# Loads of u and v in runs of 1024 B instead of 2048 B, and the turn of u in two transfers

## The chip, the cores and the metric

The kernel runs on one core of one Trainium2 chip. A core has TensorE (PE, matrix products into PSUM), VectorE (DVE), ScalarE (ACT), GpSimd (POOL) and SyncE (SP), and sixteen DMA engines that move data between the chip's memory (DRAM here) and SBUF. SP, ACT and POOL issue transfers, each into a queue of its own; the profile calls SP's queue q1, ACT's q10 and POOL's q0. The metric is the device time of one execution in microseconds (us), the median of several runs. A profile shows one such execution.

## The reference

The inputs are u and v (8 x 3136 x 256), z (8 x 3136 x 64), three projections of 256 columns in one matrix, a filter (3136 x 256) and an output matrix. All are float32. For each of the 8 batches:

```
scores = z @ z.T / 3136
x      = u * (relu(scores)**2 @ v)
x1, x2, x3 = x @ w_proj            # 256 columns each
x2c    = irfft(rfft(x2) * rfft(filter))   # along the 3136 rows
out    = (x1 * x2c * x3) @ w_out
```

The 3136 x 3136 weights of each batch are by far the largest product.

## The kernel before

The 3136 rows of a batch are taken as 64 x 49, so that the Fourier transform falls into two stages. They are held as 25 row blocks of 128 rows (the last of 64), two of the 49 columns to a block. The output rows of a batch are worked on in seven chunks of 512, 512, 512, 512, 512, 256 and 320 columns (4, 4, 4, 4, 4, 2 and 3 row blocks); 8 batches make 56 chunks.

For each chunk TensorE makes scores of pairs of row blocks against the chunk into PSUM (from zT_t), ACT or DVE applies relu (into R_t) and the square (into A_t), and TensorE weighs v with A_t. The sums go to PSUM, where DVE multiplies them with u, turned, into xT_t (L1975). Scores are symmetric: a block of weights that a later chunk needs is not made again but turned. SP issues a transposing transfer (DMA_TRANSPOSE) from A_t to M_t, M2e_t or M2o_t (L1848), and a later chunk weighs with those. An A_t is free when its turn and its products are done.

From xT_t come the three projections. The middle one goes through the Fourier stages by way of DRAM: SP stores s_t and gs_t to the spectrum buffers and loads them again (spec_in_t, conv_in_t). At the end of a batch the gates, the convolution and the output matrix give ost_t, which SP stores to out_dram.

The loads: u, v and z come from DRAM as float32 and are cast to bfloat16 by the transfer itself. Only POOL issues such loads. A load fills 64 of the 128 partitions, one for each of 64 row groups, with up to four row blocks side by side. `load_rows` (L644) does it for v, into a tile v_t that holds the 25 blocks of one batch, 256 columns each; `v_at` (L641) is the column of a block, with 16 unused columns between chunks. `cast_u` (L627) does it for u, one chunk at a time, into un_t, with `cast_rows` (L618). Each chunk has two loads of u, one for each half of the partitions, and two pieces of v of the next batch. Each of them follows a small copy on POOL into `tick`, which waits for a given piece of work, so that loads are spread over time. u is loaded two chunks ahead.

The turn of u: SP issues one transposing transfer per chunk from un_t to uT_t (`load_uT`, L1561, issued at L1565), which DVE reads at the end of the chunk. uT_t and un_t have two buffers each, M_t one, M2e_t and M2o_t one each, A_t eight.

The order of the work comes from a planner that runs when the program is built. It takes costs and due times for each task; the order of TensorE's work and the choice between ACT and DVE are written out in two strings. [...]

Of the kernel before, what the change touches and what calls it, by code (L numbers as in the profile page):

```python
# [11 lines left out]
P = 128  # L12
F32 = mybir.dt.float32
BF16 = mybir.dt.bfloat16
# [4 lines left out]
N1 = 64  # L19
# [367 lines left out]
def kernel(  # L387
# [10 lines left out]
    nc = tc.nc  # L398

    B, S, D = u.shape  # L400
# [3 lines left out]
    NT = (N2 + 1) // 2  # L404
    NC = len(CHUNKS)
    C0 = [sum(CHUNKS[:i]) for i in range(NC)]
    QUART = S // 4
    T0 = [x // P for x in C0] + [NT]
    tiles = [list(range(T0[c], T0[c + 1])) for c in range(NC)]
    home = {t: c for c in range(NC) for t in tiles[c]}  # L410
    VW = NT * D + 16 * (NC - 1)
    inv_s2 = 1.0 / float(S) ** 2
    h_scale = 2.0 / float(S)

# [23 lines left out]
    PS = bass.MemoryType.PSUM  # L438
    zT_p = Pool("zT", 2, [P, NT * P], BF16)
    uT_p = Pool("uT", 2, [P, 4, 2, P], BF16)  # L440
    un_p = Pool("un", 2, [P, 4, D], BF16)
    zn_p = Pool("zn", 1, [P, 8, dqk], BF16)
    zd_p = Pool("zd", 1, [P, 8, 2, dqk], BF16)
    v_p = Pool("v16", 2, [P, VW], BF16)
    R_p = Pool("R", 3, [P, 2, 512], F32)
# [130 lines left out]
    def on(engine, emit, cost, deps=(), takes=(), **kw):  # L576
        return job(None, lambda e: emit(), {engine: cost}, deps, takes, **kw)
# [18 lines left out]
    def rows_n1(x):  # L596
        return x.rearrange("(n1 n2) d -> n1 n2 d", n2=N2)

    def runs(lo, hi):
        got = []  # L600
        for c in range(NC):
            a, b = max(lo, T0[c]), min(hi, T0[c + 1])
            if a < b:
                got.append((0, a, b, NT - T0[c + 1] + a - T0[c]))
        if lo < min(hi, NT - 1):
            got.append((1, lo, min(hi, NT - 1), NT + lo))
        return got
# [10 lines left out]
    def cast_rows(t, src, t0, t1, twice=False, js=(0, 1)):  # L618
        x = rows_n1(src)
        if twice and t1 == NT:  # L620
            nc.gpsimd.dma_start(out=t[N1:P, t1 - 1 - t0, :], in_=x[:, END_N2, :])
        for j, lo, hi, n2 in runs(t0, t1):
            if j not in js:
                continue
            nc.gpsimd.dma_start(out=t[ds(j * N1, N1), lo - t0 : hi - t0, :], in_=x[:, n2 : n2 + hi - lo, :])  # L625

    def cast_u(b, c, js=(0, 1)):  # L627
        if 0 in js:
            u_nat[b, c] = un_p.tile()
        t = u_nat[b, c]  # L630
        if c == NC - 1 and 0 in js:
            nc.gpsimd.memset(t[N1:P, T0[c + 1] - 1 - T0[c], :], 0.0)
        cast_rows(t, u[b], T0[c], T0[c + 1], js=js)

    def await_x(xt):
        nc.gpsimd.tensor_copy(tick[:], xt["t"][0:1, 1, 0:1])
# [2 lines left out]
        nc.gpsimd.tensor_copy(tick[:], live[un][0:1, 0:1])  # L639

    def v_at(t):  # L641
        return t * D + 16 * home[t]

    def load_rows(t, src, t0, t1, js=(0, 1)):  # L644
        r = rows_n1(src)
        for j, lo, hi, n2 in runs(t0, t1):
            if j not in js:
                continue
            for c in range(home[lo], home[hi - 1] + 1):
                a, b = max(lo, T0[c]), min(hi, T0[c + 1])  # L650
                nc.gpsimd.dma_start(  # L651
                    out=t[ds(j * N1, N1), ds(v_at(a), (b - a) * D)],
                    in_=r[:, n2 + a - lo : n2 + b - lo, :].rearrange("p t d -> p (t d)"),
                )
        if t1 == NT and 1 in js:
            nc.gpsimd.dma_start(out=t[N1:P, ds(v_at(NT - 1), D)], in_=r[:, END_N2, :])

    def row(t, i):
        return t[:, ds(v_at(i), D)]
# [6 lines left out]
    for t0, t1 in zip(z_cuts, z_cuts[1:]):  # L666
        for j, lo, hi, n2 in runs(t0, t1):
            (nc.scalar if j else nc.sync).dma_start(
                out=zf[lo // ZF][ds(j * N1, N1), lo % ZF : lo % ZF + hi - lo, :], in_=zr[:, n2 : n2 + hi - lo, :]
# [28 lines left out]
    nc.gpsimd.iota(k0v[:, 0:25], pattern=[[N1, 25]], base=0, channel_multiplier=0)  # L698
    nc.gpsimd.iota(k0v[:, 25:50], pattern=[[-N1, 25]], base=S // 2, channel_multiplier=0)
    load_rows(v16[0], v[0], 0, 8)  # L700
    u_nat = {}
    load_rows(v16[0], v[0], 8, 16)
    cast_u(0, 0)
    load_rows(v16[0], v[0], 16, NT)
    wp16 = const.tile([P, 2, 3 * D], BF16, name="wp16")
    nc.gpsimd.dma_start(out=wp16[:], in_=moe_w_proj.rearrange("(t p) n -> p t n", p=P))
    cast_u(0, 1)
    wo16 = const.tile([P, 2, D], BF16, name="wo16")
    S2_AT = 30.0
# [40 lines left out]
    def after(task, at):  # L750
        task.ready = max(task.ready, at)
        return task
# [12 lines left out]
    for i, (t0, t1) in enumerate(zip(z_cuts, z_cuts[1:])):  # L765
        step_ = -(-(t1 - t0) // -(-(t1 - t0) // 8))
        for g0 in range(t0, t1, step_):
# [15 lines left out]
            n = nt * dqk  # L783
# [6 lines left out]
            w = min(nt * P, S - g0 * P)  # L790
# [367 lines left out]
    def c_quads(i, n=1):  # L1158
        return n * (1 if i else 2) * c_pe(2 * D) + 0.01
# [4 lines left out]
    def add_quads(mm, ev, cost, deps, takes, wide=True):  # L1164
        box = {}

        def go():
            box["p"] = take_pair()
            mm(box["p"])

        a = pe("Q", go, cost, deps, [pair_slots, *takes])
        evs = []
        for h in ((0, 1),) if wide else (0, 1):
            x = slice(0, 2) if wide else slice(h, h + 1)
            e_ = job(None, lambda e, x=x: ev(e, x, box["p"][:, x, :]), both(2 * D * (1 + wide)), [a])
            e_.frees.append((a, 0))
            evs.append(e_)
        a.holders = len(evs)
        return a, evs
# [18 lines left out]
    for j0 in range(0, NJ, 4):  # L1198
        ld, ibox = load_spec(DF, j0, 4, puts, LATE_F)
        for i in range(2):  # L1200
# [7 lines left out]
            a, evs = add_quads(mm, ev, c_quads(j0 // 2 + i), [*s2_done, ld], [])  # L1208
# [340 lines left out]
    uT = {}  # L1549
# [8 lines left out]
    def u_tiles(c):  # L1558
        return -(-CHUNKS[c] // P)

    def load_uT(b, c, deps):  # L1561
        def go():
            uT[b, c] = uT_p.tile()
            n = -(-CHUNKS[c] // P)
            nc.sync.dma_start_transpose(  # L1565
                out=uT[b, c][:, 0:n].rearrange("p t h j -> p (t h) j"),
                in_=u_nat[b, c][:, 0:n].rearrange("p t d -> p (t d)"),
            )

        made = cu[b, c]  # L1570
        if not isinstance(made[0], Task):
            t = after(on("SP", go, 1.3, deps, [uT_p.slots], moves=0.2 * u_tiles(c), late=LATE_U), made[1])
            t.frees.append((Held(un_p.slots, made[0]), 0))
        else:
            t = on("SP", go, 1.3, [*deps, *made], [uT_p.slots], moves=0.2 * u_tiles(c), late=LATE_U)
            t.frees.append((made[0], 0))
        t.clogs = True
        u_tasks[b, c] = t
# [17 lines left out]
    def casts_at(b, c):  # L1596
# [60 lines left out]
        if x < len(slots):  # L1657
            box = []

            def go_u(tick_, js):  # L1660
                a = on(
                    "POOL", lambda: cast_u(*slots[x], js), 0.55 * len(js), [tick_, *box], [] if box else [un_p.slots],
                    moves=0.264 * len(js) * u_tiles(slots[x][1]), late=LATE_CAST,
                )
                box.append(a)
                if 1 in js:
                    cu[slots[x]] = box[0], a
                    load_uT(*slots[x], [])

            got += [lambda t_, j=j: go_u(t_, (j,)) for j in range(2)]  # L1670
# [48 lines left out]
    def parts(un):  # L1719
        b, c, k = un  # L1720
        pair = plans[b, c][k][1]
        return [(t, c) for t in pair] + ([(NT - 1, SHARE[c])] if c in SHARE and pair == (NT - 1,) else [])
# [157 lines left out]
    for gi, g in enumerate(groups):  # L1880
        deps = []
        for un in g:
            b, c, k = un
            if b == 0:
                hi = max((plans[b, c][k][1][-1] + 1) * P, C0[c] + CHUNKS[c])
# [19 lines left out]
        for i, un in enumerate(g):  # L1905
            b, c, k = un
            cw = CHUNKS[c]
            pair = plans[b, c][k][1]
            rows, n = P, len(parts(un))
# [54 lines left out]
            if last:  # L1964
# [48 lines left out]
                if calls or b == 0 and c < 3:  # L2013
# [8 lines left out]
                    for i, call in enumerate(calls):  # L2022
                        k = (i * (len(mine) + 1)) // len(calls) if mine else 0
# [6 lines left out]
    for gi, got in ends_at.items():  # L2030
        for b, c in got:
            q_, un, _ = short[b, c]
# [37 lines left out]
```

## Time and profile before

| | |
|---|---|
| time, median of 3 runs | 951.24 us (949.6 to 953.36) |
| the profiled execution, its own time | 946.01 us |
| its span, first to last instruction | 944.1 us |
| mean granted TensorE clock | 0.997 |
| TensorE, DVE, ACT, POOL busy | 97%, 89%, 87%, 26% of the span |
| packets in flight, q1 and q0 | 70.1% and 26.4% of sixteen DMA engines' time |
| moved by DMA | 170.70 MB, mean 181 GB/s |

Lines of the profile name the kernel's line, the engine, what is written and read, the count, the busy time and mean length, and the idle time of the engine just ahead with what ended it. "SPq" is an issue of a transfer by SP: the time for which SP was taken up, not the transfer's own. "The chain" follows the work that ended last back to the start. In the lines on transfers "KB" is one transfer's size in SBUF, and the last number the median time from issue to landing. Shares of the DMA queues add up the times of all packets; packets overlap on an engine, so they can exceed 100%.

### The profile page before, as it was taken

How to read it: one execution, taken by the hardware profiler on the slowest of the kernel's cores; microseconds unless marked ns; L12 is line 12 of the kernel's file. 1: busy time of each engine (PE TensorE's matmuls, PEld its weight loads, DVE VectorE, ACT ScalarE, POOL GpSimd, SP SyncE). 2: the span in 40 equal slices, each digit the busy share in tenths (PEclk: the TensorE clock that was granted, in tenths of full speed). 3: DMA queues.
4: the chain of work that ended last, by engine and by line, in shares of the span. 5: the costliest groups of instructions: out<-in, count | busy, mean ns of one | idle time of the engine just before them, and what ended most of it. 6: DMA issues, size and time to landing. Idle time of an engine off the chain costs nothing.

```text
span 944.1 us, 30298 instructions
## 1 busy us (share of the span) xinstructions
PE 914.1 (97%) x12423; PEld 557.1 (59%) x12423; DVE 838.5 (89%) x1116; ACT 819.7 (87%) x953; POOL 248.8 (26%) x585
## 2 busy tenths in 40 slices
PE   8999999999999999999999999999999999999986
PEld 3446565566555666556665665666665666666654
DVE  8987899998888998999888988989988999899785
ACT  7968988999889988888989998889988999899573
POOL 5244223231322322223121321333123140101030
PEclk9999999999999999999999999999999999999999
DMA  9999799978999889998899989999889989897867
GB/s 155 162 181 181 117 179 184 181 150 182 170 217 201 146 181 192 209 156 159 190 183 215 176 155 200 173 184 174 183 172 207 221 138 196 193 216 132 193 189 241
DMA packets 331643, 170.70 MB, mean 181 GB/s; under 512 B 242886, under 2 KB 307142, under 8 KB 331504
## 3 DMA queue, kind: packets, MB, share of 16 engines
q1 hardware_dynamic: 301624, 131.98, 70.1%
q0 software_dynamic: 29168, 35.13, 26.4%
q8 instruction: 97, 1.59, 0.7%
q10 hardware_dynamic: 712, 1.66, 0.6%
q14 instruction: 42, 0.34, 0.1%
HBM read 90.26 MB, written 53.05 MB: 152 GB/s over the span
## 4 chain that ended last, share of the span: by engine, by line
PE 77%; DMA 10%; DVE 6%; ACT 3%; issue 2%; SPq 1%; POOL 0%; ACTq 0%; DVEq 0%; POOLq 0%
PE ps_s L516 77%; DMA M_t<-A_t 4%; DMA out_dram<-ost_t 1%; ACT R_t L1919 1%; DMA M_t<-spec_in_t 1%; DVE xh L1357 1%; ACT A_t L1928 1%; DVE yT_t L1462 1%; DVE A_t L1930 1%; DMA v_t<-spec 1%; DMA spec<-gs_t 1%; DMA M2e_t<-A_t 1%; ACT gs_t L582 1%; DVE R_t L1357 1%; DMA spec_in_t<-spec 0%
## 5 line engine op out<-in xcount | busy, mean ns | idle before, releaser
L516 PE MATMUL ps_s<-A_t,v_t 64*128 64x512 bf16 (+5 forms) x4766 | 516.1, 352 | 0.9 <-DVE A_t L1930 0.7
L516 PEld LDWEIGHTS <-v_t 64*128 64x128 bf16 (+1 forms) x6528 | 306.4, 98 | 187.7 <-PE ps_s L516 19.3
L1919 ACT ACTIVATE R_t<-ps_s 128x1024 f32<-128x1024 f32 (+3 forms) x359 | 336.9, 962 | 47.4 <-PE ps_s L516 43.8
L1928 ACT ACTIVATE A_t<-R_t 128x1024 bf16<-128x1024 f32 (+2 forms) x281 | 271.8, 993 | 15.3 <-DMA M_t<-A_t 6.3
L1930 DVE SCALAR_TENSOR_TENSOR A_t<-R_t 128x1024 bf16<-128x1024 f32 (+3 forms) x211 | 233.6, 1123 | 21.6 <-ACT R_t L1919 12.1
L516 PE MATMUL ps_s<-zT_t 64*128 64x512 bf16 (+5 forms) x1186 | 192.2, 351 | 3.6 <-DVE gate_t L1256 2.1
L1921 DVE TENSOR_SCALAR R_t<-ps_s 128x1024 f32<-128x1024 f32 (+4 forms) x153 | 170.2, 1123 | 20.9 <-PE ps_s L516 10.4
L639 POOL COPY tick<-A_t 1x1 bf16<-1x1 bf16 x159 | 56.2, 354 | 428.0 <-ACT A_t L1928 264.2
L516 PE MATMUL ps_s<-xT_t,wp 64*128 64x512 bf16 (+3 forms) x976 | 124.7, 352 | 0.1
L516 PE MATMUL ps_s<-M_t,v_t 64*128 64x512 bf16 (+4 forms) x860 | 97.2, 353 | 3.2 <-DMA M_t<-A_t 2.4
L516 PEld LDWEIGHTS <-zT_t 64*128 64x128 bf16 (+1 forms) x1219 | 69.1, 97 | 51.7 <-issue 8.2
L582 ACT ACTIVATE x_t<-ps_s 128x1024 bf16<-128x1024 f32 (+3 forms) x75 | 69.5, 928 | 22.8 <-PE ps_s L516 22.5
L1357 DVE TENSOR_TENSOR xh<-xh,H 128x1024 bf16<-128x1024 bf16 x120 | 81.7, 685 | 2.3 <-ACT xh L582 1.4
L1256 DVE TENSOR_TENSOR gate_t<-ps_s,x_t 128x512 bf16<-128x512 f32 (+2 forms) x112 | 64.4, 617 | 12.4 <-PE ps_s L516 9.0
L1462 DVE TENSOR_TENSOR yT_t<-ps_s,gate_t 128x1024 bf16<-128x1024 f32 (+2 forms) x53 | 56.9, 1078 | 14.3 <-PE ps_s L516 14.1
L1975 DVE TENSOR_TENSOR xT_t<-ps_s,uT_t 128x512 bf16<-128x512 f32 (+2 forms) x112 | 64.0, 613 | 6.3 <-PE ps_s L516 5.8
L516 PEld LDWEIGHTS <-wp 64*128 64x128 bf16 (+1 forms) x976 | 48.0, 96 | 29.7 <-PE ps_s L516 2.0
L516 PE MATMUL ps_s<-wp,xT_t 64*128 64x256 bf16 (+2 forms) x944 | 64.2, 266 | 0.8 <-ACT R_t L1919 0.7
L516 PE MATMUL ps_s<-wo,yT_t 64*128 64x256 bf16 (+2 forms) x904 | 62.1, 266 | 2.2 <-DVE yT_t L1462 1.0
L625 POOL DMA_DIRECT2D un_t<-in_u_dram x112 | 57.9, 518 | 17.4 <-issue 15.6
L651 POOL DMA_DIRECT2D v_t<-in_v_dram x112 | 58.2, 524 | 14.1 <-issue 10.4
L516 PEld LDWEIGHTS <-xT_t 64*128 64x128 bf16 (+1 forms) x944 | 44.1, 97 | 19.3 <-issue 1.5
(156 smaller groups left out, 905.7 us busy)
## 6 DMA issues: line engine op xcount, KB each, us to landing
out_dram<-ost_t SPq DMA_DIRECT2D x60, 256.0 KB
spec_in_t<-spec SPq DMA_DIRECT2D x56, 192.0 KB
spec<-gs_t SPq DMA_DIRECT2D x56, 192.0 KB
v_t<-in_v_dram POOLq DMA_DIRECT2D x80, 128.0 KB, 4.8
un_t<-in_u_dram POOLq DMA_DIRECT2D x80, 128.0 KB, 4.4
spec<-s_t SPq DMA_DIRECT2D x40, 256.0 KB
conv_in_t<-spec SPq DMA_DIRECT2D x34, 256.0 KB
out_dram<-ost_t SPq DMA_DIRECT2D x18, 128.0 KB
```

The costliest lines, as they stand in the source:

```text
L516: got = nc.tensor.matmul(o, *args, **kw)
L582: got = nc.scalar.activation(out_, in_, AF.Copy)
L625: nc.gpsimd.dma_start(out=t[ds(j * N1, N1), lo - t0 : hi - t0, :], in_=x[:, n2 : n2 + hi - lo, :])
L651: nc.gpsimd.dma_start(out=t[ds(j * N1, N1), ds(v_at(a), (b - a) * D)], in_=r[:, n2 + a - lo : n2 + b - lo, :].rearrange("p t d -> p (t d)"),)
L1256: has_read(nc.vector.tensor_tensor(o[:, :, ::-1] if h == 0 else o, p, x, ALU.mult), p)
L1357: nc.vector.tensor_tensor(x[:, 1 - i], x[:, 0], h, ALU.mult)
L1462: has_read(nc.vector.tensor_tensor(yb["y"][:, :, 0:w], p, gates[b, c][:, :, 0:w], ALU.mult), p)
L1919: has_read(nc.scalar.activation(r, p, AF.Relu), p)
L1921: has_read(nc.vector.tensor_single_scalar(r, p, 0.0, ALU.max), p)
L1928: nc.scalar.activation(a, r, AF.Square, scale=1.0 / float(S))
L1930: nc.vector.scalar_tensor_tensor(a, r, inv_s2, r, ALU.mult, ALU.mult)
L1975: has_read(nc.vector.tensor_tensor(x[:, :, ::-1] if h == 0 else x, f, ut, ALU.mult), f)
```

## The change

The tile of a chunk of u, un_t, is now two groups of two row blocks with 16 unused columns after each group. The tile of v gets 16 unused columns after every second row block of a chunk. A load of four row blocks is still one transfer, but its run in SBUF is broken after two blocks: two runs of 512 bfloat16 elements, 1024 B, in each partition. The memory side is cut in the same way. Three row blocks now take two transfers, one of two blocks and one of one block. The turn of u works on one group at a time: two transfers for chunks of four or three row blocks, one for the chunk of two. The strings and the planner's costs are the same; so is the order of the instructions on TensorE, ACT and DVE.

```diff
-    VW = NT * D + 16 * (NC - 1)
+    starts = sorted(t for c in range(NC) for t in tiles[c][::2])
+    pads = {t: sum(x <= t for x in starts) - 1 for t in range(NT)}
+    VW = NT * D + 16 * len(starts)
...
-    un_p = Pool("un", 2, [P, 4, D], BF16)
+    un_p = Pool("un", 2, [P, 2, 2 * D + 16], BF16)
...
+    def u_part(t, lo, n):
+        return t[:, lo // 2, ds(lo % 2 * D, n * D)]
+
     def cast_u(b, c, js=(0, 1)):
...
-        cast_rows(t, u[b], T0[c], T0[c + 1], js=js)
+        x = rows_n1(u[b])
+        for j, lo, hi, n2 in runs(t0, T0[c + 1]):
+            if j not in js:
+                continue
+            k = (hi - lo) // 2
+            if k:
+                nc.gpsimd.dma_start(
+                    out=t[ds(j * N1, N1), 0:k, 0 : 2 * D],
+                    in_=x[:, n2 : n2 + 2 * k, :].rearrange("p (k t) d -> p k (t d)", k=k),
+                )
+            if (hi - lo) % 2:
+                nc.gpsimd.dma_start(out=u_part(t, hi - 1 - t0, 1)[ds(j * N1, N1)], in_=x[:, n2 + hi - lo - 1, :])
...
     def v_at(t):
-        return t * D + 16 * home[t]
+        return t * D + 16 * pads[t]
...
-                nc.gpsimd.dma_start(
-                    out=t[ds(j * N1, N1), ds(v_at(a), (b - a) * D)],
-                    in_=r[:, n2 + a - lo : n2 + b - lo, :].rearrange("p t d -> p (t d)"),
-                )
+                while a < b:
+                    m = 1 if (a - T0[c]) % 2 else min(2, b - a)
+                    k = max(1, (b - a) // 2) if m == 2 else 1
+                    out = t[ds(j * N1, N1), ds(v_at(a), k * (2 * D + 16))] if k > 1 else t[ds(j * N1, N1), ds(v_at(a), m * D)].unsqueeze(1)
+                    if k > 1:
+                        out = out.rearrange("p (k w) -> p k w", k=k)[:, :, 0 : 2 * D]
+                    nc.gpsimd.dma_start(
+                        out=out,
+                        in_=r[:, n2 + a - lo : n2 + a - lo + k * m, :].rearrange("p (k t) d -> p k (t d)", k=k),
+                    )
+                    a += k * m
...
-            nc.sync.dma_start_transpose(
-                out=uT[b, c][:, 0:n].rearrange("p t h j -> p (t h) j"),
-                in_=u_nat[b, c][:, 0:n].rearrange("p t d -> p (t d)"),
-            )
+            for k in range(0, n, 2):
+                m = min(2, n - k)
+                nc.sync.dma_start_transpose(
+                    out=uT[b, c][:, k : k + m].rearrange("p t h j -> p (t h) j"), in_=u_part(u_nat[b, c], k, m)
+                )
```

POOL at the start of the program, where v and u of the first batch are loaded ahead of the projections' matrix (wp), before and then now. A form like 64x1024 is partitions by elements; 64x2x512 is two runs of 512 elements in each partition. Counts at the end of a row are repeats.

```order
L651 DMA v_t<-in_v_dram 64x1024 x8
L625 DMA un_t<-in_u_dram 64x1024 x2
L651 DMA v_t<-in_v_dram 64x1024
L651 DMA v_t<-in_v_dram 64x512
L651 DMA v_t<-in_v_dram 64x768
L651 DMA v_t<-in_v_dram 64x1024
```

```order
L674 DMA v_t<-in_v_dram 64x2x512 x8
L645 DMA un_t<-in_u_dram 64x2x512 x2
L674 DMA v_t<-in_v_dram 64x2x512
L674 DMA v_t<-in_v_dram 64x512 x2
L674 DMA v_t<-in_v_dram 64x256
L674 DMA v_t<-in_v_dram 64x2x512
```

The order is the same; the load of 768 elements is now one of 512 and one of 256.

SP in the sixth batch, where a turn of u stands ahead of a store of s_t, two stores of the output and two turns of weights into M_t, before and then now. For a DMA_TRANSPOSE 128x8x128 is eight squares of 128 x 128, that is four row blocks of 256 columns.

```order
L1620 DMA_TRANSPOSE zT_t<-zd_t 128x8x128
L1565 DMA_TRANSPOSE uT_t<-un_t 128x8x128
L1028 DMA spec_1_60<-s_t 128x4x256
L1511 DMA out_dram<-ost_t 64x1024 x2
L1848 DMA_TRANSPOSE M_t<-A_t 128x8x128 x2
```

```order
L1645 DMA_TRANSPOSE zT_t<-zd_t 128x8x128
L1591 DMA_TRANSPOSE uT_t<-un_t 128x4x128 x2
L1052 DMA spec_1_60<-s_t 128x4x256
L1535 DMA out_dram<-ost_t 64x1024 x2
L1873 DMA_TRANSPOSE M_t<-A_t 128x8x128 x2
```

Nothing has changed its place; one more transfer stands ahead of the rest.

SP at the last turn of u, that of the last chunk, with the stores of the last spectrum but one ahead and the loads of the next one behind, before and then now.

```order
L1406 DMA spec_0_61<-gs_t 48x2048 x2
L1406 DMA spec_0_61<-gs_t 2x2048
L1565 DMA_TRANSPOSE uT_t<-un_t 128x6x128
L1077 DMA spec_in_t<-spec_1_60 40x2048 x4
L1091 DMA conv_in_t<-spec_0_61 128x4x256 x2
```

```order
L1430 DMA spec_0_61<-gs_t 48x2048 x2
L1430 DMA spec_0_61<-gs_t 2x2048
L1591 DMA_TRANSPOSE uT_t<-un_t 128x4x128
L1591 DMA_TRANSPOSE uT_t<-un_t 128x2x128
L1101 DMA spec_in_t<-spec_1_60 40x2048 x4
L1115 DMA conv_in_t<-spec_0_61 128x4x256 x2
```

The turn of three row blocks has become one of two blocks and one of one block, at the same place.

More of the change, by code (lines that the diff above doesn't have):

```diff
@@ L630, in cast_u @@
         t = u_nat[b, c]
+        t0 = T0[c]
         if c == NC - 1 and 0 in js:
-            nc.gpsimd.memset(t[N1:P, T0[c + 1] - 1 - T0[c], :], 0.0)
-        cast_rows(t, u[b], T0[c], T0[c + 1], js=js)
+            nc.gpsimd.memset(u_part(t, T0[c + 1] - 1 - t0, 1)[N1:P], 0.0)
+        x = rows_n1(u[b])
[10 more added lines that the diff above has]
+                nc.gpsimd.dma_start(out=u_part(t, hi - 1 - t0, 1)[ds(j * N1, N1)], in_=x[:, n2 + hi - lo - 1, :])
     def await_x(xt):
```

## The prediction

> **What bounds the kernel now.** I read the page first: busy shares, the two DMA queues, and the shares of the chain of waits.
>
> ```profile
> span 944.1 us, 30298 instructions
> PE 914.1 (97%) x12423; PEld 557.1 (59%) x12423; DVE 838.5 (89%) x1116; ACT 819.7 (87%) x953; POOL 248.8 (26%) x585
> ...
> q1 hardware_dynamic: 301624, 131.98, 70.1%
> q0 software_dynamic: 29168, 35.13, 26.4%
> ...
> PE 77%; DMA 10%; DVE 6%; ACT 3%; issue 2%; SPq 1%; POOL 0%; ACTq 0%; DVEq 0%; POOLq 0%
> PE ps_s L516 77%; DMA M_t<-A_t 4%; DMA out_dram<-ost_t 1%; ACT R_t L1919 1%; DMA M_t<-spec_in_t 1%; DVE xh L1357 1%; ACT A_t L1928 1%; DVE yT_t L1462 1%; DVE A_t L1930 1%; DMA v_t<-spec 1%; DMA spec<-gs_t 1%; DMA M2e_t<-A_t 1%; ACT gs_t L582 1%; DVE R_t L1357 1%; DMA spec_in_t<-spec 0%
> ```
>
> TensorE bounds it: 914.1 of 944.1 us busy, so all of its idle time together is 30.0 us. A change of loads can win at most part of that, and can lose more. Second comes the DMA: 26.4% and 70.1% of sixteen engines' time are packets in flight, and 10% of the chain, 94 us, are transfers. The casting loads are the smaller queue, q0, which GpSimd issues; the turns, the spectrum and the output go through q1, nearly all issued by SP.
>
> Then the chain in order of time (start, length, what), for the places where a transfer ends last.
>
> ```profile
> 17.57 10.96 DMA M_t<-spec_in_t
> ...
> 279.66 5.55 DMA out_dram<-ost_t
> ...
> 377.49 7.05 DMA M_t<-A_t
> ...
> 393.83 5.95 DMA out_dram<-ost_t
> 399.80 7.75 DMA M_t<-A_t
> ...
> 619.18 8.86 DMA M_t<-A_t
> ...
> 638.34 5.61 DMA spec<-gs_t
> ...
> 880.09 1.33 SPq L1565
> ...
> 884.00 4.56 DMA spec_in_t<-spec
> ```
>
> None of them is a load of u or v. They are what SP issues: turns of weights (M_t), spectra and outputs. So the loads matter through what they do to SP's transfers, and the turn of u (L1565) matters as something that stands in SP's queue ahead of these. In the row at 880.09 it is on the chain itself.
>
> **The change part by part.** It edits three things: the runs of the loads, their number on POOL, and the number of turns on SP.
>
> (1) Shorter runs. How the loads are issued (count, KB each, median us to landing), and what one stretch with long runs and one with shorter runs moved (q0: packets, MB, share of the sixteen engines; the first row is for 11 to 13 us, the second for 13 to 16 us, where q0 is nearly alone):
>
> ```profile
> v_t<-in_v_dram POOLq DMA_DIRECT2D x80, 128.0 KB, 4.8
> un_t<-in_u_dram POOLq DMA_DIRECT2D x80, 128.0 KB, 4.4
> v_t<-in_v_dram POOLq DMA_DIRECT2D x8, 96.0 KB, 4.2
> un_t<-in_u_dram POOLq DMA_DIRECT2D x8, 96.0 KB, 3.8
> ```
>
> ```profile
> q0 software_dynamic: 241, 0.40, 107.0%
> ```
>
> ```profile
> q0 software_dynamic: 517, 0.53, 105.7%
> ```
>
> Each 128 KB load fills 64 partitions with a run of 2048 B; now it is two of 1024 B. Each 96 KB load becomes 1024 and 512 B. That adds 160 x 64 + 16 x 64 = 11,264 runs. The price of one more run, from the two stretches: 1.070 x 16 x 2 us / 241 = 142 ns a packet at 0.40 MB / 241 = 1.66 KB, and 1.057 x 16 x 3 us / 517 = 98 ns at 1.03 KB. The line through both is 70 ns per KB and 26 ns per packet. By it the change adds 11,264 x 26 ns / 16 = 18.3 us of all sixteen engines, 1.9% of the span. From below the price is nothing, if time goes by bytes alone.
>
> [...]
>
> Where this lies on the path: mostly nowhere, since loads land 4 to 5 us after issue and are asked for two chunks ahead, and a chunk is 944.1 / 56 = 16.9 us. Without that cover the 18.3 us would count whole. There are two exceptions. At the start ten such loads of v, four of u and one of 96 KB are issued ahead of 17.57, where the chain waits 10.96 us for a turn: 15 x 64 x 26 ns / 16 = 1.6 us at most, 0 at least. I take **1.0**, nearer the measured line. And the chain's 94 us of transfers, slowed by 1.9% at most, lose 0 to 1.8; I take **0.5**, since most of them are issued while few loads are in flight.
>
> (2) Sixteen more loads on POOL (each 96 KB one is split in two). They take 16 x 0.518 us by the first row below, 8.3 us. POOL is busy 26%, so I count nothing; without that idle time it would be the 8.3.
>
> ```profile
> L625 POOL DMA_DIRECT2D un_t<-in_u_dram x112 | 57.9, 518 | 17.4 <-issue 15.6 <-DVE xT_t L1975 0.7 <-DVE xh L1362 0.3
> ...
> L1975 DVE TENSOR_TENSOR xT_t<-ps_s,uT_t 128x512 bf16<-128x512 f32 (+2 forms) x112 | 64.0, 613 | 6.3 <-PE ps_s L516 5.8
> ```
>
> The second row is the only reader of uT_t: of its 6.3 us of waiting 5.8 are for TensorE, none is put down to a turn. So a turn of u that ends later costs its reader nothing.
>
> (3) The turn of u is two transfers in 48 of 56 cases (all chunks but the one of 256 columns). SP issues in order. What a short turn costs it: the turn at 865.28 is that of the chunk of 256 columns, as large as the first half of the new ones.
>
> ```profile
> 865.28 1.20 SPq L1565 DMA_TRANSPOSE uT_t<-un_t  x1
> ...
> 881.53 2.80 SPq L1077 DMA_DIRECT2D spec_in_t<-spec  x4
> ```
>
> The half turn takes 1.20 us where the one at 880.09, of three row blocks, takes 1.33: the issue is nearly a fixed price. With the 0.09 us that SP needs between two instructions a split adds 1.3 us, 48 x 1.3 = 62 us of SP's time. Behind each stand whatever SP issues next: turns of weights, spectra, outputs. The delay ends at SP's next pause. In the last row the spectrum's loads come right behind the turn at 880.09, and the chain goes through both: **1.3** us at the end, with little doubt.
>
> In the middle I looked at SP's timeline ahead of the chain's transfers:
>
> ```profile
> 275.94 1.40 SPq L1565 DMA_TRANSPOSE uT_t<-un_t  x1
> 277.44 4.15 SPq L1511 DMA_DIRECT2D out_dram<-ost_t  x4
> ```
>
> ```profile
> 391.51 1.28 SPq L1565 DMA_TRANSPOSE uT_t<-un_t  x1
> 392.89 1.55 SPq L1511 DMA_DIRECT2D out_dram<-ost_t  x2
> ```
>
> ```profile
> 614.04 2.42 SPq L1565 DMA_TRANSPOSE uT_t<-un_t  x1
> 616.55 0.54 SPq L1028 DMA_DIRECT2D spec<-s_t  x1
> 617.19 1.87 SPq L1511 DMA_DIRECT2D out_dram<-ost_t  x2
> 619.18 5.71 SPq L1848 DMA_TRANSPOSE M_t<-A_t  x2
> ```
>
> ```profile
> 630.74 2.35 SPq L1565 DMA_TRANSPOSE uT_t<-un_t  x1
> 633.19 0.53 SPq L1028 DMA_DIRECT2D spec<-s_t  x1
> 633.78 2.06 SPq L1511 DMA_DIRECT2D out_dram<-ost_t  x2
> 635.93 1.93 SPq L1062 DMA_DIRECT2D spec_in_t<-spec  x3
> 637.96 1.40 SPq L1406 DMA_DIRECT2D spec<-gs_t  x3
> ```
>
> In all four SP goes from a turn that is split now to the chain's transfer with gaps of about 0.1 us, so 1.3 us more ahead should reach it. The bounds are 0 and 4 x 1.3 = 5.2. At 391.51 the output right behind is the one whose landing releases the turn at 399.80: all 1.3. [...] At 275.94 the chain's own piece is a later output of the four and may have waited for data: 0.65. Together **3.25**.
>
> The sum: 1.3 + 1.0 + 0.5 + 3.25 = 6.05 us. The profiled execution took 946.0 us (its span and 1.9 around it) and the median of the runs shown is 951.24, 5.2 more. So 946.0 + 6.05 = 952.1 for an execution like it, and **957.3** for the median. With all lower ends 951.24 + 1.3 = 952.5; with all upper ends 951.24 + 1.3 + 1.6 + 1.8 + 5.2 = 961.1.
>
> **The rivals.**
>
> *Faster: loads stop holding up the turns.* Busy times, clock, DMA share and GB/s of two stretches of the start:
>
> ```profile
> 15.00:20.00 5.00, 5.00 (x47) 2.23 (x46) 5.00 (x9) 4.96 (x7) 1.94 (x5) 1.00 1.31 115
> ...
> 25.00:30.00 5.00, 4.22 (x40) 1.68 (x38) 4.06 (x5) 4.94 (x6) 1.09 (x3) 1.00 1.08 196
> ```
>
> While loads and turns are in flight together (15 to 20 us) only 115 GB/s get through; with the loads done it is 196. If half as long a run lets a turn in earlier, the start gains: the 5 us at a rate midway, 155, save 5 x (1 - 115 / 155) = 1.3 us. The M_t pieces of the chain, 4% or some 40 us, may shrink by a fifth, 8. Less the 1.3 of the end that is 8.0: 951.24 - 8.0 = 943.2. It decides from where the turns gain more than SP loses, 6 us. Against it: the bytes are the same, q0 has but 26.4 of 96.5 points of the engines' time, and the four places where SP comes late stay. [...] Chance 0.20.
>
> *No change: SP's pauses take the 62 us.* Only the 1.3 of the end and half of the start stay, 1.8: 953.0. For it: SPq is 1% of the chain. Against it: the four places above have no pause. Chance 0.28.
>
> *Much slower: the DMA engines become the bound* and the 18.3 us count whole, with the end 19.6: 970.8. For it: 96.5% of their time is taken. Against it: packets overlap (shares above 100% stand in the rows), and no load of u or v is on the chain. Chance 0.07.
>
> **How the numbers follow.** The forecast has 0.45, its own range 952.5 to 961.1. Half a percent, about what a measurement here can tell from no change, is 4.8 us: below 946.5, above 956.0. Of the forecast I put 0.36 above 956.0 and 0.09 below; with the last rival slower has 0.43; same has 0.09 + 0.28 = 0.37; faster 0.20. The range is 945 to 966: it leaves out over half of the first rival and most of the last, under 0.2 together.
>
> **What would show it.** Right: 104 turns of uT_t with a median near 1.2; POOL with 16 more issues of unchanged length; q0 with about 11,000 more packets and a larger share at the same MB; TensorE's idle time up by some 6 us, behind M_t, outputs or spectra, with two turns of u back to back ahead of them on SP; the first M_t of the chain landing near 29.5 instead of 28.5; and at the end 1.3 us more ahead of the last spectrum loads. Wrong: q0's packet count unchanged (runs joined again); shorter M_t pieces on the chain with SP as late as forecast; q0's share up by 5 points or more; or waits of L1975 for the turn of u.

## The result and the profile after

The changed kernel took 960.38 us in the median of 4 runs (955.51 to 962.48), the kernel before 950.42 (946.04 to 953.36): a ratio of 1.0111, 95% interval 1.0071 to 1.0151. It is slower by about 1%, and 957.3 had been predicted. Measured twice more, with more runs, the ratio was 1.0086 (1.0050 to 1.0122) and 1.0104 (1.0066 to 1.0142). Ratios here and below are of fast executions alone, those within 1.5% of the fastest of their kernel, while the medians of the experiments are over all.

The profiled execution after took 958.36 us (span 956.5), the one before 946.01 (span 944.1): 12.4 us more span. Single executions of one kernel scatter by 5 us and more to either side of their median, so what follows tells where this pair of executions differs; what each part of the change costs is for the experiments, and they place the loss of the split turns elsewhere than this pair does.

The page of the kernel after: busy times, DMA queues, shares of the chain.

```profile
span 956.5 us, 30370 instructions
PE 920.0 (96%) x12423; PEld 559.4 (58%) x12423; DVE 839.7 (88%) x1116; ACT 819.9 (86%) x953; POOL 269.1 (28%) x601
...
q1 hardware_dynamic: 303160, 131.99, 70.8%
q0 software_dynamic: 40688, 35.13, 29.2%
...
PE 80%; DMA 8%; DVE 6%; ACT 3%; issue 2%; SPq 1%; POOL 0%; ACTq 0%; DVEq 0%; POOLq 0%
```

The queue q0 has 11,520 packets more at the same bytes: 11,264 are the added runs, and 256, sixteen to each of the 16 added loads, are packets of 4 B (5,638 of that size in the trace before, 5,894 after). So the runs were really cut. POOL issues 16 loads more, but its busy time grows by 20.3 us, not by 8.3. The groups of costliest instructions and the lines that read or write uT_t tell why, and what a turn costs SP (minimum, median, maximum in ns):

```profile
L645 POOL DMA_DIRECT2D un_t<-in_u_dram x112 | 64.3, 575 | 27.3 <-issue 22.3 <-DMA v_t<-in_v_dram 1.5 <-DMA xh<-in_moe_filter_fft_dram 1.0
```

```profile
L1591 SPq DMA_TRANSPOSE uT_t<-un_t x104: 1173/1257/2879, 15.0 to 892.8; - x104
...
  DVE xT_t L2000: 0.9, 1
```

The mean issue of a load of u on POOL rose from 518 ns to 575. That mean is over 80 loads with two runs in each partition, 599 ns each, and 32 with one run, as before, 516 ns each. The 104 turns have a median of 1.257 us; the 56 before had 1.288 for up to twice the data. So the issue price of a turn is nearly fixed at the median; all turns of u together took SP 144.1 us instead of 90.5. The reader of uT_t waited for a turn once, for 0.9 us.

Now the pieces of the chain that answer to those shown before, in order of time:

```profile
21.12 7.55 DMA M_t<-spec_in_t
28.71 33.77 PE ps_s L518 x326
...
287.85 5.86 DMA M_t<-A_t
...
296.31 26.98 PE ps_s L518 x382
...
410.82 6.65 DMA M_t<-A_t
417.52 39.10 PE ps_s L518 x526
...
891.27 1.37 SPq L1591
892.75 1.66 SPq L1591
894.47 0.39 issue
894.86 0.29 SPq L1101
```

At the start next to nothing is lost: the turn lands at 21.12 + 7.55 = 28.67; before, the same turn landed at 17.57 + 10.96 = 28.53. In this pair the loss lies in the middle, around turns of weights into M_t. At the end the last turn of u begins at 891.27 instead of 880.09, which is 11.2 us late, and the loads behind it begin at 894.86 instead of 881.53, 13.3 us late. So 0.1 us is lost at the start, some 11.1 in the middle, 2.1 in the tail, and 0.9 is won back behind it: 12.4.

The 11.1 us of the middle have two parts. The first is plain idle time of TensorE. Two stretches of 420 us, before and then after (length, TensorE's busy time, granted clock, DMA share, GB/s):

```profile
30.00:450.00 420.00, 414.61 (x5386) 1.00 1.00 175
450.00:870.00 420.00, 414.61 (x5823) 1.00 0.99 183
```

```profile
30.00:450.00 420.00, 408.62 (x5284) 0.99 1.04 171
450.00:870.00 420.00, 413.00 (x5713) 1.00 1.03 184
```

Idle time rises from 10.8 to 18.4 us, by 7.6. The second part is in the clock column. Windows of 3 us of the kernel after, at two of its long stalls:

```profile
293.00:296.00 3.00, 0.00 (x0) 1.00 1.18 302
296.00:299.00 3.00, 2.69 (x24) 0.77 1.01 230
299.00:302.00 3.00, 3.00 (x26) 0.66 1.33 146
413.00:416.00 3.00, 0.68 (x20) 1.00 1.55 157
416.00:419.00 3.00, 1.48 (x20) 0.69 1.08 215
419.00:422.00 3.00, 3.00 (x64) 0.75 0.83 163
```

TensorE sits idle for 3.51 and 3.84 us and then runs on at a lower clock, 0.50 for 3.41 us in the trace's clock records at both places. A window's clock is the mean over its whole length, so (1 - 0.77) x 3 + (1 - 0.66) x 3 = 1.7 us are lost at the first place and as much at the second, where the first 0.4 us of the lower clock still fall into the stall (the clock falls at 417.11, the products begin at 417.52). 7.6 + 3.4 = 11.0, which is the middle's loss. The chain shows the first of the two as well. Before, the products behind that stall were

```profile
293.01 25.32 PE ps_s L516 x382
```

and after, the same 382 begin at 296.31 and take 26.98, 1.7 more. TensorE is counted as busy meanwhile. That is 3.4 of the 5.9 us by which its busy time rose, from 914.1 to 920.0, for the same 12423 products; the rest lies before 30 us and behind the last turn of u. In the middle of the execution before there was no such dip.

The second stall is a wait for a turn of weights. The products that read it, with the wait ahead of them, before and then after:

```profile
408.65 0.63 PE L516 MATMUL ps_s<-M_t,v_t 64*64 64x512 bf16 x8 [0.75 <-DMA M_t<-A_t]
```

```profile
417.52 1.07 PE L518 MATMUL ps_s<-M_t,v_t 64*64 64x512 bf16 x8 [3.84 <-DMA M_t<-A_t]
```

What ACT waited for, out of the view of waits (us in total, times, longest), before and then after:

```profile
ACT A_t L1928 <- DMA M_t<-A_t: 6.3, 5, 2.0
```

```profile
ACT A_t L1953 <- DMA M_t<-A_t: 12.7, 6, 5.0
```

These waits for turns of weights have doubled. An A_t that is not turned yet is not free, so ACT cannot write the next weights. And SP, ahead of the stall at 413 us:

```profile
398.84 3.61 SPq L1591 DMA_TRANSPOSE uT_t<-un_t  x2
402.56 1.25 SPq L1535 DMA_DIRECT2D out_dram<-ost_t  x2
403.93 2.00 SPq L1430 DMA_DIRECT2D spec<-gs_t  x3
406.02 2.37 SPq L1086 DMA_DIRECT2D spec_in_t<-spec  x3
408.49 0.39 SPq L1052 DMA_DIRECT2D spec<-s_t  x1
408.93 4.54 SPq L1873 DMA_TRANSPOSE M_t<-A_t  x2
```

From the split turn to the turn of weights there is no gap of more than 0.15 us. The place is the one that the prediction showed at 391.51. There the turn took 1.28 us; now its two halves take 3.61.

### The profile page after: what moved, and what is told of

Same layout as the page of the kernel before. It is cut to its first block, busy times and chain, and to the rows that moved or that the text cites. A ratio compares the mean times of both kernels' runs of the same rounds, so it can differ in the third digit from the quotient of the medians.

```text
span 956.5 us, 30370 instructions
## 1 busy us (share of the span) xinstructions
PE 920.0 (96%) x12423; PEld 559.4 (58%) x12423; DVE 839.7 (88%) x1116; ACT 819.9 (86%) x953; POOL 269.1 (28%) x601
## 3 DMA queue, kind: packets, MB, share of 16 engines
q0 software_dynamic: 40688, 35.13, 29.2%
q10 hardware_dynamic: 712, 1.66, 0.6%
## 4 chain that ended last, share of the span: by engine, by line
PE 80%; DMA 8%; DVE 6%; ACT 3%; issue 2%; SPq 1%; POOL 0%; ACTq 0%; DVEq 0%; POOLq 0%
PE ps_s L518 80%; DMA M_t<-A_t 5%; DVE xh L1381 1%; ACT R_t L1944 1%; DMA M_t<-spec_in_t 1%; ACT A_t L1953 1%; DMA M2e_t<-A_t 1%; DVE gate_t L1280 1%; DMA conv_in_t<-spec 1%; DVE A_t L1955 1%; DVE yT_t L1486 1%; DVE R_t L1381 1%; SPq L1086 0%; DVE xT_t L2000 0%; SPq L1591 0%
## 5 line engine op out<-in xcount | busy, mean ns | idle before, releaser
L674 POOL DMA_DIRECT2D v_t<-in_v_dram x120 | 68.7, 578 | 12.9 <-issue 10.0
L645 POOL DMA_DIRECT2D un_t<-in_u_dram x112 | 64.3, 575 | 27.3 <-issue 22.3
```

The lines of the kernel that those rows point to most:

```text
L645: nc.gpsimd.dma_start(out=t[ds(j * N1, N1), 0:k, 0 : 2 * D], in_=x[:, n2 : n2 + 2 * k, :].rearrange("p (k t) d -> p k (t d)", k=k),)
L674: nc.gpsimd.dma_start(out=out, in_=r[:, n2 + a - lo : n2 + a - lo + k * m, :].rearrange("p (k t) d -> p k (t d)", k=k),)
```

## The experiments

The theory to be tested (A): the loss is the issue time of 48 more turns in SP's queue. Its rivals: the shorter runs cost DMA time or make the loads faster; the unused columns cost something of their own. Each ratio is against the kernel before on the same chip.

**Two turns, loads as before.** The kernel before with nothing but the split:

```diff
-            nc.sync.dma_start_transpose(out=uT[b, c][:, 0:n]..., in_=u_nat[b, c][:, 0:n]...)
+            for k in range(0, n, 2):
+                m = min(2, n - k)
+                nc.sync.dma_start_transpose(out=uT[b, c][:, k : k + m]..., in_=u_nat[b, c][:, k : k + m]...)
```

> Loads as before, the turn of u in two transfers as in the change: 48 more issues on SP, no more packets of loads. Theory A (SP's queue carries the loss: the terms 1.3 at the end and 3.25 in the middle): 4 to 6 us slower than before. Theory B (the shorter runs load the DMA engines and carry it): within 2 us of before. If the loss is both together and nearly additive, this and the kernel with short runs alone add up to about the 10 us of the change.

955.98 us, ratio 1.0069 (1.0033 to 1.0106). The split alone makes the kernel slower.

**Short runs, one turn.** The kernel before with its loads cut into runs of 1024 B, without unused columns. Both sides of a load are walked in reversed order, so that neighbouring runs stay apart (the queue has 40,688 packets, as in the change):

```diff
+ out=t[ds(j * N1, N1), at : at + n, :].rearrange("p (k t) d -> p k (t d)", k=q)[:, ::-1],
+ in_=x[:, n2 + at : n2 + at + n, :].rearrange("p (k t) d -> p k (t d)", k=q)[:, ::-1],
```

> Runs of 1024 B for u and v (the two runs of a transfer in reversed order, so that they aren't joined; no unused columns), each turn of u one transfer: SP issues as before, about 11,500 more packets on q0. Theory A (SP's queue): 1 to 2 us slower than before (the terms 1.0 and 0.5). Theory B (DMA engines): 7 to 10 us slower, with q0's share near 29% as in the change and turns of weights landing later.

946.76 us, ratio 0.9979 (0.9948 to 1.0011). **Runs of 512 B**, by the same edit with one row block to a run:

> Runs of 512 B for u and v (reversed order as in the kernel with runs of 1024 B), each turn of u one transfer: some 36,000 more packets on q0, three times the change. Theory A: 3 to 5 us slower. Theory B: 20 us slower or more, q0's share above 33%.

948.39 us, ratio 0.9997 (0.9965 to 1.0028). The loads' queue in the pages of these two:

```profile
q0 software_dynamic: 40688, 35.13, 28.1%
```

```profile
q0 software_dynamic: 65008, 35.13, 30.3%
```

The packets are there, and they take time: 28.1% of 945.3 us is 265.6, 16.4 more than before, times 16 engines over 11,264 runs = 23 ns a run. In packets: one of 2048 B took 173 ns at the median before, one of 1024 B 98 ns here, so two of them take 23 ns more. The kernel's time shows none of it, not even with three runs added to a load of four blocks. So shorter runs neither cost nor help here, within the 0.3% of these intervals.

**Four turns.** As the first, with a turn for each row block, 144 turns more than before:

```diff
-            for k in range(0, n, 2):
-                m = min(2, n - k)
+            for k in range(0, n, 1):
+                m = min(1, n - k)
```

> Loads as before, the turn of u one transfer for each row block: 144 more issues on SP where the change has 48. Theory A: the loss of the two-transfer kernel grows about threefold, 12 to 18 us. Theory B: within 3 us of before.

1017.2 us, ratio 1.0721 (1.0660 to 1.0781). Three times the extra turns cost 10 times as much as in the first experiment. The chain's shares, the turns of u, and the same two stretches of 420 us as above:

```profile
PE 57%; DMA 16%; ACT 8%; SPq 7%; DVE 6%; issue 5%; POOL 0%; ACTq 0%; DVEq 0%; POOLq 0%
```

```profile
L1567 SPq DMA_TRANSPOSE uT_t<-un_t x200: 1167/1242/2930, 13.9 to 946.6; - x100
```

```profile
30.00:450.00 420.00, 393.99 (x4979) 0.98 0.94 163
450.00:870.00 420.00, 394.87 (x5378) 0.99 0.95 171
```

A quarter of the data still takes 1.242 us to issue. TensorE's idle time in the middle is 51.1 us (10.8 before), and SP itself is 7% of the chain. Added up over the rows of SP's issues in the traces, SP is taken up for 671 of 944 us before, 721 of 957 after the change, and 839 of 1012 here: 71%, 75% and 83%. My reading is that between stretches of work SP catches up while there are pauses, and that with 83% the pauses no longer suffice; no run fills SP in steps between 75% and 83%.

**Plain issues in place of turns.** The kernel before, with two small transfers by SP behind each of the 48 turns that the change splits. They store 4 KB each to a scratch buffer, which is work beside the computation:

```diff
+            for k in range(2 if n > 2 else 0):
+                at = ((b * NC + c) * 2 + k) * 16
+                nc.sync.dma_start(out=DX[at : at + 16, :], in_=ident[0:16, :])
```

> Before, with two plain transfers of 4 KB from a constant to scratch memory behind each of the 48 turns of three or four row blocks: the second half's time on SP (2 x about 0.55 us) with no transposing transfer more. If SP's time in its queue is what costs: 4 to 7 us slower than before, as with two turns. If it is the second transposing transfer's own work or start on the DMA engines: within 2 us of before.

952.81 us, ratio 1.0042 (1.0007 to 1.0077). The 96 issues:

```profile
L1572 SPq DMA_DIRECT2D aside<-ident x96: 402/568/1312, 16.0 to 881.8; - x96
```

Added up they are 52 us of SP, close to the 56 by which the turns of u grew with two turns. But SP's other issues, its stores of the output above all, took less time in this execution, so that SP is taken up for 704 us, 33 more than before, where two turns make it 721, 50 more. The loss is of the same order, and the interval overlaps that of two turns. So plain issues on SP cost something, if barely clear of the noise, without any turn being split; what the 96 small transfers cost as transfers was not tried apart. That a turn costs no more than plain issues of the same length is not shown; the intervals are too wide.

**Less work on SP.** The kernel before, with the output stores of the first six batches issued by POOL:

```diff
- s_ = on("SP", lambda nt=nt, store=store: store(0, nt), 1.1, ...
+ s_ = on("SP", lambda nt=nt, store=store: store(0, nt, by=nc.gpsimd), 1.1, ...
```

> Before, with the stores of the output of the first six batches issued by POOL instead of SP at the same points of the plan: about 66 issues of 0.6 us, 40 us, less on SP. If SP's queue is what holds the kernel back in its stalls: 3 to 8 us faster than before. If only what stands right ahead of a turn of weights counts, or POOL's loads now wait behind a store: within 3 us, or slower.

948.39 us, ratio 0.9990 (0.9951 to 1.0029). POOL has 84 instructions more, SP 84 less, SP is taken up for 630 us instead of 671, and nothing is gained. The simplest reading is that SP as it stands before is not what limits the kernel and becomes a cost when work is added. But the stores waited on POOL for 108 us in all (before, with eight stores there, 37), mostly for ACT, and POOL's loads stand behind them; that a loss there hid a gain on SP is not excluded.

**The change without its unused columns, and the change again.** Two turns with the reversed short runs of above; and the change as it is:

> Runs of 1024 B (reversed order, no unused columns) and the turn in two transfers: the change without its unused columns. If the loss is only SP's extra issues: 5 to 8 us slower than before, as with two turns alone (1.0069), and the repeated change the same. If the unused columns, by which every second part starts 32 B further, cost something of their own: this one 3 us or more faster than the repeated change.

952.92 us, ratio 1.0038 (1.0008 to 1.0067).

> The change itself once more, beside the others on one chip: 7 to 14 us slower than before (1.0111 measured first). If the loss above the two turns alone (1.0069) was chance it comes down to 6 to 8 us.

956.93 us, ratio 1.0086 (1.0050 to 1.0122). The two intervals overlap, but the means of the executions behind the two ratios are 3.6 us apart, with a 95% interval of 1.0 to 6.2. Four kernels on one more chip were to tell whose columns these are. The first is the change without unused columns again:

> The short runs of u and of v written in reversed order, no unused columns, every turn in two: the change without its unused columns, a second time, beside the three kernels below on one chip. Theory A (the loss is the 48 extra turns on SP's queue, the unused columns are nothing): as the first time, ratio 1.004 to 1.008, and the change itself and both halves below land within 0.003 of it. Theory B (the unused columns cost about 5 us of their own): 1.003 to 1.005 here, and the kernel or kernels below with the guilty columns at 1.008 to 1.011.

953.64 us, ratio 1.0064 (1.0031 to 1.0097).

The second has u as in the change, v in reversed runs with the old columns:

```diff
-    VW = NT * D + 16 * len(starts)
+    VW = NT * D + 16 * (NC - 1)
-        return t * D + 16 * pads[t]
+        return t * D + 16 * home[t]
```

> The change with the unused columns behind u's second row block alone; v's runs reversed, without unused columns. If it is the source of the second turn, which starts 32 B off, that costs: 1.008 to 1.011, and the half turns of this kernel are longer to issue than the others', by some 5 us over 48. If v's columns cost: 1.003 to 1.005. If the columns are nothing (theory A): within 0.003 of the kernel with none.

955.04 us, ratio 1.0070 (1.0035 to 1.0105). The columns of u cost nothing that can be told.

The third has v as in the change, u in reversed runs without columns, its turn in two:

```diff
-    un_p = Pool("un", 2, [P, 2, 2 * D + 16], BF16)
+    un_p = Pool("un", 2, [P, 4, D], BF16)
```

> The change with the unused columns behind v's row blocks alone; u's runs reversed, its turn in two, without unused columns. If it is v's other addresses (which TensorE reads as its 64-row weights and moving data) that cost: 1.008 to 1.011, and matmuls or weight loads that read v are longer by about 5 us over all. If u's columns cost: 1.003 to 1.005. If the columns are nothing (theory A): within 0.003 of the kernel with none.

960.76 us, ratio 1.0134 (1.0092 to 1.0176). And the change a third time:

> The change as it is, on the same chip as the three above. Earlier: 1.0111 (1.0071 to 1.0151) and 1.0086 (1.0050 to 1.0122). Theory A: 1.004 to 1.010 and within 0.003 of the kernel without unused columns. Theory B: 1.008 to 1.011, 0.004 or more above the kernel without them, and the two halves add up to it.

958.39 us, ratio 1.0104 (1.0066 to 1.0142). Over all chips the four measurements with v's new columns lie at 1.0086 to 1.0134, the four with split turns and without them at 1.0038 to 1.0070. On the last chip the means of the medians are 959.6 and 954.3: 5.2 us between them (by the means of the executions 4.9, interval 2.3 to 7.4). So theory A explains somewhat over half of the loss (the four without v's columns average 1.0060, 5.7 us); v's new layout brings about 5 more. Layout, because two things go with the columns: later tiles lie further on (below), and in three of the four kernels without them v's runs are walked in reverse. Short runs of v walked forward without columns were not tried.

**Where each kernel loses.** TensorE does the same 12,423 products in every kernel, in the same order but for near neighbours. I numbered them by their start, and took from each trace the time from product 501 (62 us before) to product 10,751 (829 us before), and from there to the end of the span:

| kernels, one profiled execution of each | 501 to 10,751 | from there to the end |
|---|---|---|
| before; runs of 1024 B; runs of 512 B; outputs by POOL | 766.8; 765.8; 764.0; 768.4 | 115.0; 116.1; 116.5; 115.9 |
| plain issues | 764.6 | 118.4 |
| turns split, v without new columns: the first, both times without any, u's alone | 770.6; 766.5; 767.8; 769.5 | 121.0; 121.0; 120.5; 119.1 |
| turns split, v's new columns: the change three times, v's alone | 777.3; 771.3; 778.3; 776.2 | 116.6; 119.5; 120.1; 121.0 |

By the means of the rows the split costs 2.4 us in the middle and 4.5 at the end. V's layout costs 7.2 more in the middle and nothing more at the end. These are single executions, so each entry can be off by some us. So the 11 us that the first pair showed in the middle are not typical of split turns: at the two long stalls the kernel with two turns alone loses nothing against the execution before. The end is where the split shows most steadily: the four kernels of the third row lose 3.2 to 5.2 us there against the mean of the first, and only the first profile of the change, with 116.6, hardly does. The chain of the kernel with two turns alone at the last turn of u:

```profile
886.52 1.27 SPq L1567
887.89 1.63 SPq L1567
889.59 0.39 issue
```

The spectrum's loads begin at 889.98, 3.46 us behind the start of the turn; before it was 1.44. TensorE then waits for conv_in_t, one of these loads: 0.2 to 0.3 us in the kernels of the first two rows, 1.1 to 3.2 in the eight with split turns.

How v's layout acts stays open. It is not the readers of v. In the groups of costliest instructions the largest group of products that read it has the same mean length (the kernel with v's columns alone, then the one with none):

```profile
L518 PE MATMUL ps_s<-A_t,v_t 64*128 64x512 bf16 (+5 forms) x4766 | 516.0, 352 | 0.6 <-DVE A_t L1955 0.3 <-ACT A_t L1953 0.2
```

```profile
L516 PE MATMUL ps_s<-A_t,v_t 64*128 64x512 bf16 (+5 forms) x4766 | 515.1, 352 | 0.9 <-DVE A_t L1947 0.7
```

On the last chip the two kernels with v's columns also had a slow stretch in the first batch. Here are 68 to 84 us of four kernels, the change a third time, v's columns alone, u's columns alone, and no columns:

```profile
68.00:84.00 16.00, 9.52 (x89) 0.89 1.51 106
```

```profile
68.00:84.00 16.00, 12.48 (x105) 0.87 1.41 129
```

```profile
68.00:84.00 16.00, 16.00 (x156) 1.00 1.19 183
```

```profile
68.00:84.00 16.00, 15.47 (x143) 1.00 1.29 183
```

With v's columns TensorE is idle for 6.5 and 3.5 us there, with more packets in flight (share 1.51 and 1.41) and fewer bytes moved (106 and 129 GB/s). It waits for a turn of weights: the chain's piece there is 15.96 and 12.44 us long, 9.69 in the kernel with none. Over the whole execution ACT's waits for such turns point the same way: 10.5 to 12.9 us in the four kernels with v's columns, 6.1 to 11.7 in the four with split turns and without them, 4.0 to 7.4 with single turns. The loads' packets are not longer at the median: 98 ns for those of 1024 B in all kernels with short runs. But in the first profile of the change the stretch is not slow, so this is not the rule for v's columns:

```profile
68.00:84.00 16.00, 15.40 (x145) 1.00 1.28 178
```

The wider tile of v also shifts every later tile in SBUF, by 2 x 7 x 32 = 448 B in each partition for its two buffers; that shift was not tried apart from the columns.

No kernel of these beats the kernel before.

## Why the prediction was right, step by step

The time was right, 957.3 predicted and 960.38 measured, and the mechanism that carried three quarters of its sum, SP's queue (1.3 + 3.25 of 6.05), is confirmed: the split alone costs about 6 us. The terms were not of the right size, and that their sum came so near is partly luck.

- *Shorter runs, the price.* The line through two stretches gave 26 ns a packet; the runs of 1024 B took 23 ns each as shares of time in flight, without turns or columns.
- *Shorter runs, the place.* The terms of 1.0 at the start and 0.5 on the chain's transfers were too large. The start lost 0.1 us, and the kernels with 11,264 and 35,840 more runs lost nothing that can be told. The sum should have had nothing here; that the cover, loads asked for two chunks ahead, hides it is the likely reason.
- *POOL.* Nothing was counted, rightly, but for issues "of unchanged length", wrongly: a load of u with two runs took 599 ns instead of 519. The cover was large enough for 20.3 us as it was for 8.3.
- *The end.* 1.3 us were forecast "with little doubt". In the profile of the change the loads begin 2.1 us later behind the turn: the second half took 1.66 us where 1.20 was taken, and 0.39 us of idle time came behind it. Over the whole end the kernels with split turns lose 4.5 us by the table, so this was the more undersized of SP's two terms. The delay does not stop at the spectrum's loads; TensorE waits longer for conv_in_t, 2.3 us in the profile of the change and 0.2 in the one before.
- *The middle.* 3.25 us were forecast from four places of 1.3 or 0.65. Of these, 0.65 each stood for the places at 614.04 and 630.74, where the turn of u had taken 2.42 and 2.35 us; no run shows what made these two turns longer than the median of 1.288, or that a second half adds half its price there. In the profile of the change the two halves took SP 4.17 and 2.56 us at these places. The kernels that split turns without v's columns lose 2.4 there by the table, about what was forecast, but not at fixed places. In the first pair 11.0 are lost, and the last two of the four places lose nothing: TensorE's products are 7.9 us late ahead of the place at 614.04 and 7.7 behind that at 630.74. Where a delay did reach TensorE in this pair, it was larger than the 1.3 allowed. Two halves took SP 3.61 us at 398.84, where 1.28 had stood; the products behind waited 3.84 us for their M_t where they had waited 0.75; and each of the two long stalls cost 1.7 more through the clock.
- *Unused columns.* The prediction did not price them. About 5 us of the result go with v's. So the agreement of 957.3 with 960.38 rests on errors of both signs: run lengths were charged 1.5 us that they do not cost, SP's turns about 1 too little, and v's columns nothing.

The rivals. *Faster, because loads let turns in earlier*, falls by the experiment made for it: short runs with one turn gave 0.9979 (0.9948 to 1.0011), where 8 us of gain would have been 0.992. *No change, because SP's pauses take it all*, falls by the split alone, 1.0069, though pauses do take most of it: 56 us more of SP's time in turns of u cost some 6. *Much slower, by the DMA engines*, falls by the runs of 512 B.

## What to carry to other kernels

Ask of an added transfer what it costs the engine that issues it, not what it moves: here a turn took 1.25 us of its issuer whether it moved one, two or four row blocks, while cutting the loads into 2.2 times the packets cost nothing that can be told. The price of a delay in SP's queue was not linear here: 48 more turns cost 0.4 to 0.7%, 144 cost 7.2%, and taking 84 issues away won nothing, so the queue's load in percent and its pauses have to be read before a delay is priced. One pair of profiles does not place a loss: here the first pair showed it in the middle, and only the traces of the other kernels told which part of it belongs to which edit. And a forecast should list every thing that an edit changes, the layout too: the columns looked like mere bookkeeping of the edit, and about half of its loss goes with them.

## What was not expected of the hardware

- After long stalls TensorE ran at a lower clock: 1.7 us lost behind each of the two above, which at half speed is 3.4 us of it. Up to the last 4 us of the span, the clock records of the kernel after have three dips, at 297.64, 417.11 and 901.80, and those of the kernel before have one, at 9.46; each stands at 0.50 and lasts 3.41 us. The three of the kernel after go with stalls of 3.51, 3.84 and 2.28 us that end at 296.31, 417.52 and 902.16. The windows of three more kernels have the same loss of 1.7 us: two windows of 3 us at 0.55 and 0.88 in the short runs with one turn (from 505 us), at 0.73 and 0.70 in the second profile of the change (from 635 us), and at 0.52 and 0.91 with v's columns alone (from 735 us). In the kernel with v's columns alone a stall of 2.32 us (the timeline's row for TensorE, then the window) was followed by a dip:

```profile
735.20 1.92 PE L518 MATMUL ps_s<-M2o_t,v_t 64*64 64x512 bf16 x16 [2.32 <-ACT R_t L1944]
```

```profile
735.00:738.00 3.00, 2.80 (x28) 0.52 1.25 161
```

  In the kernel before, a stall of 2.07 us had no dip behind it:

```profile
293.01 0.39 PE L516 MATMUL ps_s<-zT_t 64*128 64x512 bf16 x2 [2.07 <-DVE gate_t L1256]
```

  In the kernel after, one of 3.04 us, ending at 640.50, had none either. So among these stalls of 2 to 3.1 us it depends on more than the length.
- A casting load of u took POOL 516 to 519 ns to issue in the mean with one run to a partition, 599 with two and 624 with four (runs of 512 B): the second run costs 80 ns, two more only 25.
- The issue of a transposing transfer had nearly the same median with turns of up to four, two and one row blocks: 1.288, 1.257 and 1.242 us.
